# Attention and FFN in one kernel: wide matmuls issued as four column quarters that share rounds with PV, with other buffer rings and another split of the exponential

## The chip, the cores and the metric

The kernel runs on one core of a Trainium2 chip. The metric is the device time of one launch in microseconds (us); the median of three runs is shown. In the profile PE is the tensor engine (matmuls), PEld its weight loads, DVE the vector engine, ACT the scalar engine, POOL a third elementwise engine, SP the engine that issues most transfers.

## The reference

For x of 2048 rows and 512 columns the kernel computes x + attention(xn) + FFN(xn), with xn the layer norm of x. Attention has 32 query heads of size 16 and one shared key and value head. The FFN has 1792 inner columns.

```
xn = layernorm(x)
q, k, v = xn @ wq, xn @ wk, xn @ wv            # 32 heads of 16; one head of 16; one of 16
o = softmax(q @ k.T / 4) @ v                   # per head, all 2048 keys
out = x + o @ wo + gelu_tanh(xn @ w1 + b1) @ w2 + b2
```

## The kernel before

**Tiles and stages.** After a prologue (layer norm, transposes, K, V, the first Q) the main loop goes over 4 blocks of 512 queries. In each block there are 8 head groups of 4 heads, and in each group 16 key tiles of 128 keys: 64 score tiles of 128 keys by 512 queries, 2,048 in all. Three tiles make a *score group* (683 groups). `scores` (L620 to L635) issues its three matmuls of 17 rows, one per head in its own row quarter of the array, into three of six PSUM banks. The banks alternate, so the scores of group u+2 have to wait until group u has been read.

**Exponential on two engines.** ACT evaluates exp for all three tiles of a group, or for two (`exp`, L640, activation at L650), into E, a ring of 12 slots. The third tile then goes to DVE, which builds the exponential as a sum of five shifted integer approximations: a first pass from PSUM (`p1`, L666) and, per batch of up to three tiles, four shifts (L680). ACT tiles give one PV matmul each, DVE tiles five.

**PV.** `pv_mm` (L669 to L672) multiplies by V, 32 columns wide: head j uses column quarter j of the array and accumulates in one PSUM bank, pO. At the end of a head group DVE copies pO out (`o_evac`, L693), small transfers on SP turn the denominators round, and DVE writes the normalized oT (L704). PV of the next group must wait for the copy.

**Side work.** Q projections of the next block (`q_group`), the first FFN matmul (`h_mm`, L744) with the GELU chain, and the output blocks (`out_tile`: 14 matmuls with w2 in `y_mm`, 8 with wo in `wo_mm`) all write PSUM bank 7 with full-array matmuls of 128 by 512 through the helper `mm` (L403). A table of `at(u, ...)` calls says behind which exponential each becomes available.

**What sets the order.** A planner (`Prog.schedule`, L109) simulates five engines with given costs and writes each engine's order down; at run time an engine takes its instructions in exactly that order, with semaphore waits. On PE it prefers what is due first, stays on PV for up to 12 matmuls (4 with scores waiting), and puts a filler, a matmul with zeros (L886), where it sees PE idle for over 0.25 us while PV is open. DVE's share is an accumulator: 0.7 of the groups, always the third tile, never in the last 7 tiles of a head group.

## Time and profile before

| | |
|---|---|
| median of three runs | 901.55 us (899.56 to 901.85) |
| profiled execution, its own time | 904.14 us |
| its span, first to last instruction | 902.4 us |
| mean granted PE clock | 0.977 |
| first exponential starts, last ends | 44.1 us, 885.7 us |
| busy: PE, ACT, DVE | 861.9, 787.2, 784.7 us |
| score matmuls | 2,048 |
| PV matmuls from E, from DVE tiles | 1,602 and 2,230 |
| exponentials on ACT of three and of two tiles | 236 and 447 |
| fillers | 101 |

Busy times are unions of an engine's instructions. Matmul ends are modelled by the profiler, so starts are the better guide on PE. A clock of 0.50 in a row means that the tensor engine was granted half of its pulses.

### The profile page before, as it was taken

The numbers are of one execution on the slowest core, as the hardware profiler recorded it, in microseconds if no ns is written. First come the engines' busy times: TensorE is split into PE (matmuls) and PEld (weight loads), VectorE is DVE, ScalarE is ACT, GpSimd is POOL, SyncE is SP. The second block draws the span as 40 slices with busy tenths as digits, with TensorE's granted clock in tenths as the row PEclk, the third lists the DMA queues.
The fourth block names the chain that finished last, engine by engine and source line by source line (L and its number), as shares of the span: only waits on it lengthen the run. The fifth ranks groups of instructions, "written<-read, shape, count | busy, mean of one in ns | idle before, by whom it ended". The sixth has DMA issues, their size and how long they took to land.

```text
span 902.4 us, 16691 instructions
## 1 busy us (share of the span) xinstructions
PE 861.9 (96%) x6893; PEld 259.5 (29%) x6893; DVE 784.7 (87%) x1498; ACT 787.2 (87%) x731; POOL 25.7 (3%) x51
## 2 busy tenths in 40 slices
PE   4799999999999999999999999999999999999997
PEld 2313322222222223233232222222222233223322
DVE  7359999989887679999998787999998777999984
ACT  3469999989898898999999988999989889999982
POOL 6030000000000000000000000000000000000000
PEclk9859999989999999999999999999999999999999
DMA  8000000000000000000000000000000000000000
GB/s 281 1 25 14 14 5 10 13 14 13 15 15 7 19 20 20 13 13 5 10 16 13 20 25 20 13 10 5 13 16 13 20 25 20 1 13 14 13 14 24
DMA packets 23958, 18.79 MB, mean 21 GB/s; under 512 B 12370, under 2 KB 19403, under 8 KB 23883
## 3 DMA queue, kind: packets, MB, share of 16 engines
q1 hardware_dynamic: 22826, 17.69, 6.6%
q8 instruction: 55, 0.90, 0.4%
q10 hardware_dynamic: 1056, 0.03, 0.1%
q14 instruction: 21, 0.16, 0.1%
HBM read 14.98 MB, written 2.35 MB: 19 GB/s over the span
## 4 chain that ended last, share of the span: by engine, by line
PE 70%; DVE 17%; ACT 12%; issue 1%; DMA 0%; DVEq 0%; ACTq 0%
PE pAll L670 30%; PE pAll L403 19%; PE pAll L633 18%; ACT E L650 10%; DVE Dt L666 5%; DVE Dt L680 5%; PE pAll L886 2%; DVE hb L748 2%; ACT xnT L493 1%; ACT ub L762 1%; DVE ub L759 1%; DVE ub L761 1%; DVE stats L452 1%; DVE Of L693 1%; DVE ub L764 0%
## 5 line engine op out<-in xcount | busy, mean ns | idle before, releaser
L650 ACT ACTIVATE E<-pAll 128x1024 bf16<-128x1024 f32 (+1 forms) x683 | 747.1, 1187 | 73.6 <-PE pAll L633 41.5
L666 DVE TENSOR_SCALAR Dt<-pAll 128x512 int16<-128x512 f32 x446 | 300.6, 686 | 77.1 <-PE pAll L633 75.2
L670 PE MATMUL pAll<-Dt,V 128*32 128x512 bf16 x2230 | 348.9, 391 | 0.1
L680 DVE TENSOR_SCALAR Dt<-Dt 128x1536 int16<-128x1536 int16 x636 | 299.0, 529 | 2.0 <-PE pAll L670 0.4
L670 PE MATMUL pAll<-E,V 128*32 128x512 bf16 x1602 | 295.4, 393 | 4.2 <-DVE Of L693 3.4
L633 PE MATMUL pAll<-QT,KT 17*128 17x512 bf16 x2048 | 267.3, 389 | 11.3 <-ACT E L650 8.7
L633 PEld LDWEIGHTS pAll<-QT,KT 17*128 17x128 bf16 x2048 | 65.9, 91 | 247.5 <-ACT E L650 147.8
L670 PEld LDWEIGHTS pAll<-Dt,V 128*32 128x32 bf16 x2230 | 94.6, 95 | 118.5 <-issue 66.6
L670 PEld LDWEIGHTS pAll<-E,V 128*32 128x32 bf16 x1602 | 70.6, 94 | 99.2 <-issue 59.0
L403 PE MATMUL pAll<-w_sb,ub 128*128 128x512 bf16 x224 | 71.0, 391 | 0.0
L403 PE MATMUL pAll<-xnT,w_sb 128*128 128x512 bf16 x224 | 66.6, 386 | 0.8 <-DVE hb L748 0.8
L748 DVE TENSOR_SCALAR hb<-pAll,b1T 128x512 bf16<-128x512 f32 x56 | 41.8, 746 | 1.3 <-PE pAll L403 1.3
L403 PE MATMUL pAll<-xnT,wqp 128*128 128x512 bf16 x128 | 40.4, 403 | 0.1
L403 PE MATMUL pAll<-wop,oT 128*128 128x512 bf16 x128 | 37.6, 383 | 2.6 <-DVE x_sb L797 1.8
L886 PE MATMUL pAll<-xnT,zeros 128*128 128x512 bf16 x101 | 35.0, 389 | 0.0
L403 PEld LDWEIGHTS pAll<-w_sb,ub 128*128 128x128 bf16 x224 | 18.1, 98 | 38.7 <-issue 29.6
L762 ACT ACTIVATE ub<-ub 128x1536 bf16<-128x1536 bf16 (+1 forms) x20 | 28.2, 1410 | 0.0
L403 PEld LDWEIGHTS pAll<-xnT,w_sb 128*128 128x128 bf16 x224 | 16.1, 97 | 34.5 <-issue 15.3
L521 DVE CAST QT<-pAll 128x512 bf16<-128x512 f32 x32 | 22.0, 688 | 1.3 <-PE pAll L403 1.0
L490 PE MATMUL pAll<-ident,ub 128*128 128x128 bf16 x64 | 9.1, 306 | 14.1 <-POOL ub L476 10.5
L693 DVE COPY Of<-pAll 128x512 f32<-128x512 f32 x31 | 21.2, 683 | 0.0
L704 DVE TENSOR_TENSOR oT<-Of,rbc 128x512 bf16<-128x512 f32 x31 | 21.2, 683 | 0.0
(91 smaller groups left out, 260.7 us busy)
## 6 DMA issues: line engine op xcount, KB each, us to landing
rbc<-rden_rows SPq DMA_DIRECT2D x124, 64.0 KB, 2.0
w_sb<-in_B_w_dram SPq DMA_DIRECT2D x2, 1792.0 KB, 12.0
x_sb<-in_A_x_dram SPq DMA_DIRECT2D x8, 256.0 KB, 4.5
out_dram<-x_sb SPq DMA_DIRECT2D x16, 128.0 KB, 1.7
ub<-in_A_wq_dram SPq DMA_DIRECT2D x1, 512.0 KB, 6.3
wop<-in_A_wo_dram SPq DMA_DIRECT2D x4, 128.0 KB, 2.8
den<-Of SPq DMA_DIRECT2D x31, 8.0 KB
rden_rows<-den SPq DMA_DIRECT2D x31, 8.0 KB, 1.4
```

The source lines that it names most:

```text
L403: return add("pe", lambda e: e.matmul(o, l, rh, start=start, stop=stop, **kw), r, w, occ=occ, lat=0.23, allow=allow)
L521: dve(lambda e: e.tensor_copy(QT[:, pq, hq, :], bank(bk)), w=[B(bk), ("QT", pq, hq)] + [("QTm", pq, hq, j) for j in range(4)], **kw)
L633: ins = e.matmul(o, l, rh, start=True, stop=True, tile_position=(q0, 0))
L650: exps.append(act(lambda e: e.activation(E[:, s0:s0 + na, :], bank(3 * x, na).rearrange("p (a n) -> p a n", a=na), ACT.Exp, scale=LN2 / 12 ...
L666: dve(lambda e: e.tensor_scalar(Dt[:, KZ, s, :], bank(bk), float(127 * 128) + SPL_D, SPL_MIN, ALU.add, ALU.max), w=[B(bk), ("D", s, KZ)], ...
L670: add("pe", lambda e, a, b: e.matmul(pO[32 * j:32 * j + 32, :], V1[:, v, kt, :], rhs, start=a, stop=b, tile_position=(0, 32 * j)), r=r + [ ...
L680: dve(lambda e, k=k: e.tensor_scalar(Dt[:, k, s0:s0 + n, :], Dt[:, KZ, s0:s0 + n, :], float(SPL_K[k]), None, ALU.add), r=[("D", s0 + i, KZ ...
L693: dve(lambda e: e.tensor_copy(Of[:, i, :], pO), w=["O", ("Of", i)], allow=0.0)
L704: onorm[gg] = dve(lambda e: e.tensor_tensor(oT[:, tb % 2, g, :], Of[:, i, :], rbc[:, i, :], ALU.mult), r=[("Of", i)] + [("rbc", i, j) for ...
L748: dve(lambda e: e.tensor_scalar(hb[:, ft % 6, :], pM, b1T[:, ft:ft + 1], None, ALU.add), r=["b1T"], w=[B(7), ("h", ft % 6)])
L762: act(lambda e: e.activation(uu, uu, ACT.Tanh, scale=GELU_K), r=uk, w=uk, n=c, allow=2.5, kind="tanh")
L886: pr.filler = lambda e: e.matmul(pO, zeros[:], xnT[:, 0, 0:TBW], start=False, stop=False, skip_group_check=True)
```

## The change

**Quarters.** A new helper `mm4` issues each wide matmul of the side work as four, each with 32 of the 128 weight columns, into its own column quarter. They have the shape of PV, are marked "side", and may stand between PV matmuls. A few (one Q group and the prologue) stay wide.

**Planner.** `pick_pe` is new: in the quarter shape it fills free quarters, goes to scores as soon as they are ready and one matmul of the visit is done, and waits 0.1 us for scores that are nearly ready. A change of shape now costs 0.1 us in the plan; latencies are a little longer. No fillers.

**Rings.** Q has one slot per head group in place of two; O is a ring of ten in place of two times eight; E has 20 slots in place of 12, the DVE tiles 8 in place of 6. Squares for the Q norm get slots of their own.

**Times of availability.** Q projections of a block come as pairs over the block before (and, for the last pair, over the block itself) with 16 sets of four small transfers in place of 6 sets; output blocks come from 3 groups on, the FFN over a longer stretch.

**Split.** Which tiles DVE takes follows a running balance of ACT and DVE load with the side work's costs; first or third tile may go, none in the last 10 of a head group.

```diff
+SWITCH = 0.1
-D_RATE = 0.7
-D_TAIL = 7
+SWITCH = 0.1
+
+ETA = 0.97
+D_LEAD = 0.0
+D_PEN = 0.3
+D_TAIL = 10
 D_FIRST = 3
-FILL_GAP = 0.25
-PV_MIN = 6
-PV_MAX = 12
-PV_S = 4
+FILL_GAP = 0
+PV_MIN = 2
+PV_S = 1
+P1_ALLOW = -20.0
+EV_ALLOW = -2.0
+S_WAIT = 0.1
+P_WAIT = 0.0
+NE_ND_KB = (20,8,3)
...
+    def pick_pe(self, t, cand, allr, mode, visit, cgbusy):
+        S = [o for o in cand if o.kind == "S"]
+        rest = [o for o in cand if o.kind != "S"]
+        nxt = min([o.rdy for o in allr if o.kind == "S"] + [t + 9.0])
+        due = lambda o: (o.rdy + o.allow, o.idx)
+        if mode == "col":
+            end = max(cgbusy)
+            if t < end - 0.01:
+                if t < end - 0.216 + 0.03:
+                    c = [o for o in rest if o.tag is not None and cgbusy[o.tag[1]] <= t]
+                    if c:
+                        return min(c, key=due)
+                return end
+            if S and visit >= PV_S:
+                return S[0]
+            if rest:
+                n = len({o.tag[1] for o in rest if o.tag})
+                if nxt - t < S_WAIT and not S and n < 4:
+                    return None
+                if n >= PV_MIN or not S:
+                    return min(rest, key=due)
+            return S[0] if S else None
+        if S:
+            return S[0]
+        if not rest or nxt - t < S_WAIT:
+            return None
+        n = len({o.tag[1] for o in rest if o.tag})
+        if n >= PV_MIN or n == 0 or min(o.rdy + o.allow for o in rest) <= t:
+            return min(rest, key=due)
+        return None
...
+                op = self.pick_pe(t, cand, ready["pe"], mode, visit, cgbusy)
+                if op is None or isinstance(op, float):
+                    free["pe"] = t + 0.03 if op is None else op
+                    continue
...
+                if op.kind in ("pv", "side"):
                     cg = op.tag[1]
                     st = max(t, cgbusy[cg], free["pe"])
                     if mode != "col":
-                        st += 0.08
+                        st = max([t, pend + SWITCH] + [c + SWITCH for c in cgbusy])
                     op.start = st
-                    cgbusy[cg] = st + 0.215
-                    op.end = st + 0.055
+                    cgbusy[cg] = st + 0.216
+                    op.end = st + 0.006
                     op.vis = st + op.occ + op.lat
                     mode = "col"
                     g = op.tag[0]
...
-    NE, ND, KB = 12, 6, 3
+    NE, ND, KB = NE_ND_KB
+    NOT = 10
...
+        def mm4(o, l, rh, start, stop, r=(), w=(), allow=1.5):
+            for j in range(4):
+                c = slice(32 * j, 32 * j + 32)
+                add("pe", lambda e, c=c, j=j: e.matmul(o[c, :], l[:, c], rh, start=start, stop=stop,
+                                                       tile_position=(0, 32 * j)),
+                    r, [(k, j) for k in w] + [k for k in w if k != B(7)], occ=0.216, lat=0.23, allow=allow, kind="side", tag=(None, j))
+
+        M4 = [(("bank", 7), j) for j in range(4)]
...
-        def q_proj(tb, hq, bk, **kw):
+        def q_proj(tb, hq, bk, f=None):
             for d in range(DT):
-                mm(bank(bk), wqp[:, d, 4 * hq:4 * hq + 4, :].rearrange("p a n -> p (a n)"),
-                   xnT[:, d, tb * TBW:(tb + 1) * TBW], d == 0, d == DT - 1, r=["wqp", ("xnT", tb)], w=[B(bk)], **kw)
+                (f or mm)(bank(bk), wqp[:, d, 4 * hq:4 * hq + 4, :].rearrange("p a n -> p (a n)"),
+                   xnT[:, d, tb * TBW:(tb + 1) * TBW], d == 0, d == DT - 1, r=["wqp", ("xnT", tb)], w=[B(bk)])
+
...
-                w=[B(bk), ("D", s, KZ)], allow=0.0, kind="p1")
+                w=[B(bk), ("D", s, KZ)], allow=P1_ALLOW, kind="p1")
...
-            onorm[gg] = dve(lambda e: e.tensor_tensor(oT[:, tb % 2, g, :], Of[:, i, :], rbc[:, i, :], ALU.mult),
-                            r=[("Of", i)] + [("rbc", i, j) for j in range(HG)], w=[("oT", tb % 2, g)], allow=3.0)
+            onorm[gg] = dve(lambda e: e.tensor_tensor(oT[:, gg % NOT, :], Of[:, i, :], rbc[:, i, :], ALU.mult),
+                            r=[("Of", i)] + [("rbc", i, j) for j in range(HG)], w=[("oT", gg % NOT)], allow=3.0)
...
         def h_mm(tb, ft):
             for d in range(DT):
-                mm(pM, w1_sb[:, d, ft * P:(ft + 1) * P], xnT[:, d, tb * TBW:(tb + 1) * TBW], d == 0, d == DT - 1,
+                mm4(pM, w1_sb[:, d, ft * P:(ft + 1) * P], xnT[:, d, tb * TBW:(tb + 1) * TBW], d == 0, d == DT - 1,
                    r=["w1", ("xnT", tb)], w=[B(7)])
             dve(lambda e: e.tensor_scalar(hb[:, ft % 6, :], pM, b1T[:, ft:ft + 1], None, ALU.add),
-                r=["b1T"], w=[B(7), ("h", ft % 6)])
+                r=["b1T"], w=M4 + [("h", ft % 6)], allow=EV_ALLOW)
...
+        def q_pair(tb, hqs, u):
+            for i, hq in enumerate(hqs):
+                at(u + 1.5 * i, lambda tb=tb, hq=hq: q_group(tb, [hq], {}), 0.93)
+            at(u + 1.5 * len(hqs), lambda tb=tb, hqs=hqs: q_m(tb, list(hqs)), 0.6)
+
+        q_pair(0, (1,), 0)
+        q_pair(0, (2, 3), 3)
+        q_pair(0, (4, 5), 10)
+        q_pair(0, (6, 7), 30)
+        at(14, b1_col)
...
-            a, b = (30, 118) if tb < NTB - 1 else (42, 112)
+                    at(u0 + 3 + 9 * i, lambda tb=tb, i=i: out_tile(tb - 1, i), 0.6)
+                q_pair(tb, (6, 7), u0 + 50)
+            a, b = (40, 165) if tb < NTB - 1 else (38, 128)
             if tb == 0:
-                a = 12
...
+                for k in range(3):
+                    q_pair(tb + 1, (2 * k, 2 * k + 1), u0 + 46 + 42.7 * k)
...
+        COST_D = 0.6 + 4 * (0.133 + 0.065 / KB)
+        load = [0.0] * (NU + 1)
+        for u, _, _, c in side:
+            load[min(NU, max(0, int(u)))] += c
+        for gg in range(1, NTB * NGR):
+            load[gg * TPG // 3] += 1.5
+        act_t, dve_t = D_LEAD, 0.0
+        par, cgn = [0, 0], [0] * HG
+        for u in range(NU):
+            dve_t += load[u]
+            ok = [t for t in (3 * u, 3 * u + 2) if t < NTILE and t % TPG < TPG - D_TAIL]
+            pen = D_PEN * (par[u % 2] - par[1 - u % 2])
+            d = bool(ok) and u >= D_FIRST and dve_t + COST_D + pen <= act_t + 0.9
+            if d:
+                t = min(ok, key=lambda t: (cgn[t % HG], -t))
+                is_d[t] = True
+                cgn[t % HG] += 1
+                par[u % 2] += 1
+                dve_t += COST_D
+            act_t += ETA * (0.904 if d else 1.331)
+            dve_t = max(dve_t, act_t - 6.0)
+        for t in range(NTILE):
+            if is_d[t]:
+                last_d[t // TPG] = t
 
```

Where the change moves work on PE, first within an output block, in the second block of queries (near score group 212). L633 and L673 are scores, L670 and L713 PV, L403 and L451 side work; `w_sb,ub` is the second FFN matmul, `wop,oT` the output projection. Before:

```order
L633 MATMUL pAll<-QT,KT 128x512 x3
L403 MATMUL pAll<-w_sb,ub 128x512
L633 MATMUL pAll<-QT,KT 128x512 x3
L403 MATMUL pAll<-w_sb,ub 128x512 x4
L670 MATMUL pAll<-Dt,V 32x512 x3
L670 MATMUL pAll<-E,V 32x512
L633 MATMUL pAll<-QT,KT 128x512 x3
```

There, full-array matmuls stand alone between scores or ahead of PV. And in the change, at the same score groups:

```order
L673 MATMUL pAll<-QT,KT 128x512 x3
L713 MATMUL pAll<-E,V 32x512
L451 MATMUL pAll<-wop,oT 32x512
L451 MATMUL pAll<-w_sb,ub 32x512 x2
L451 MATMUL pAll<-wop,oT 32x512
L713 MATMUL pAll<-Dt,V 32x512
L713 MATMUL pAll<-E,V 32x512
L451 MATMUL pAll<-wop,oT 32x512
L713 MATMUL pAll<-E,V 32x512
L713 MATMUL pAll<-Dt,V 32x512
```

Between two scores everything now has the one shape 32x512, side work and PV mixed.

The second place is PE at the end of a head group late in the first block of queries (near score group 151), where PV of the next group waits for the copy of pO. Before (`hb,sel8R` is the Q norm):

```order
L633 MATMUL pAll<-QT,KT 128x512 x3
L403 MATMUL pAll<-hb,sel8R 32x512 x2
L633 MATMUL pAll<-QT,KT 128x512 x3
L403 MATMUL pAll<-hb,sel8R 32x512 x3
L633 MATMUL pAll<-QT,KT 128x512 x3
L670 MATMUL pAll<-E,V 32x512 x4
L633 MATMUL pAll<-QT,KT 128x512 x6
L670 MATMUL pAll<-E,V 32x512 x4
```

In the change:

```order
L673 MATMUL pAll<-QT,KT 128x512 x3
L713 MATMUL pAll<-Dt,V 32x512 x2
L713 MATMUL pAll<-E,V 32x512 x3
L673 MATMUL pAll<-QT,KT 128x512 x15
L713 MATMUL pAll<-E,V 32x512
L673 MATMUL pAll<-QT,KT 128x512 x3
L713 MATMUL pAll<-E,V 32x512 x5
L713 MATMUL pAll<-Dt,V 32x512 x6
```

Five score groups stand there with no other matmul between them, in place of two.

The third place is ACT from score group 125 or so on. Before:

```order
L650 ACTIVATE E<-pAll 128x1024 x4
L650 ACTIVATE E<-pAll 128x1536
L650 ACTIVATE E<-pAll 128x1024 x3
L650 ACTIVATE E<-pAll 128x1536 x2
L650 ACTIVATE E<-pAll 128x1024 x4
```

In the change, over the same groups:

```order
L692 ACTIVATE E<-pAll 128x1536 x3
L692 ACTIVATE E<-pAll 128x1024 x4
L692 ACTIVATE E<-pAll 128x1536 x5
L692 ACTIVATE E<-pAll 128x1024 x2
L692 ACTIVATE E<-pAll 128x1536
```

Three-tile evaluations (1536) come in longer runs, and there are more of them.

More of the change, by code (lines that the diff above doesn't have):

```diff
@@ L128, in schedule @@
         visit = 0
+        pend = 0.0
         accn = {}
@@ L206, in schedule @@
                     op.vis = op.end + op.lat
-                    mode = "row" if op.kind == "S" else "full"
+                    if m == "col":
+                        cgbusy = [op.end] * 4
+                    mode = m
             else:
@@ L634, in fn @@
                 return ins
-            return add("pe", fn, r, [B(3 * x + i) for i in range(3)], occ=0.32, lat=0.18, allow=-1.0, kind="S")
+            return add("pe", fn, r, [B(3 * x + i) for i in range(3)], occ=0.216, lat=0.22, allow=-1.0, kind="S")
         eptr = [0]
```

167 lines of the change are left out of this document (73 added, 94 removed).

## The prediction

> **What bounds the kernel now.** I read the page's first part, then the timeline of the tensor engine, then stretches of the main loop.
>
> ```profile
> span 902.4 us, 16691 instructions
> PE 861.9 (96%) x6893; PEld 259.5 (29%) x6893; DVE 784.7 (87%) x1498; ACT 787.2 (87%) x731; POOL 25.7 (3%) x51
> ```
>
> PE looks busy for 96% of the span, but its ends are modelled, so I price it by starts. In the timeline, columns are start, length, engine, line, operation, count:
>
> ```profile
> 408.47 0.39 PE L633 MATMUL pAll<-QT,KT 17*128 17x512 bf16 x3
> 408.79 0.39 PE L670 MATMUL pAll<-Dt,V 128*32 128x512 bf16 x1
> 408.85 0.40 PE L670 MATMUL pAll<-E,V 128*32 128x512 bf16 x3
> 409.18 0.39 PE L633 MATMUL pAll<-QT,KT 17*128 17x512 bf16 x3
> 409.50 0.39 PE L886 MATMUL pAll<-xnT,zeros 128*128 128x512 bf16 x1
> 409.82 0.39 PE L670 MATMUL pAll<-Dt,V 128*32 128x512 bf16 x1
> ...
> 897.27 1.47 PE L403 MATMUL pAll<-wop,oT 128*128 128x512 bf16 x6 [0.79 <-DVE x_sb L797]
> ```
>
> Six matmuls of one shape take 1.47 us: (1.47 - 0.39) / 5 = 0.216 us from start to start. That is one round of the array. Three score matmuls (17 rows each), or four PV matmuls of four different column quarters, share one round. Each change of shape (score, full array, quarter) costs more: score at 408.47, quarter at 408.79, that is 0.32, and score, full, quarter at 409.18, 409.50, 409.82 again 0.32 each. So a change costs 0.32 - 0.216 = 0.10 us.
>
> With these two prices I counted the built program's order in 32 stretches of 21 score groups (672 of 683 groups). PE needs 672 score rounds, 1,363 quarter rounds (3,790 tiles; quarters that come unevenly leave holes) and 748 full rounds, with 1,598 changes: 2,783 x 0.216 + 1,598 x 0.10 = 760.9 us. The other two engines I price by instructions that follow without a gap:
>
> ```profile
> L650 ACT ACTIVATE E<-pAll 128x1024 bf16<-128x1024 f32 x5 | 4.7, 1073 | 0.0
> ```
>
> ```profile
> L650 ACT ACTIVATE E<-pAll 128x1536 bf16<-128x1536 f32 x4 | 5.5, 1458 | 0.0
> ```
>
> ```profile
> 128.25 1.96 DVE L680 TENSOR_SCALAR Dt<-Dt 128x1536 int16<-128x1536 int16 x4
> ...
> 410.23 1.29 DVE L666 TENSOR_SCALAR Dt<-pAll 128x512 int16<-128x512 f32 x2
> ```
>
> An exponential of two tiles takes (4.7 - 1.07) / 4 = 0.91 us of ACT, one of three (5.5 - 1.46) / 3 = 1.35; I use 0.92 and 1.33, within the rounding of 4.7 and 5.5. On DVE a shift of three tiles takes (1.96 - 0.55) / 3 = 0.47 us and a first pass 1.29 - 0.69 = 0.60. By stretch, I set the largest of the three needs against the time from one stretch's first exponential to the next's. Rows of eight stretches (window, length, then busy time by engine, PEclk after POOL):
>
> ```profile
> 306.60:333.00 26.40, 26.40 (x219) 7.79 (x211) 21.14 (x41) 23.07 (x23) 0.00 (x0) 1.00 0.07 22
> 668.50:691.20 22.70, 21.70 (x190) 6.08 (x187) 19.14 (x38) 22.70 (x23) 0.00 (x0) 1.00 0.06 16
> 99.60:123.60 24.00, 24.00 (x204) 7.26 (x202) 23.31 (x44) 22.80 (x23) 0.00 (x0) 1.00 0.05 14
> 44.10:75.90 31.80, 29.83 (x186) 6.44 (x184) 21.48 (x40) 24.32 (x22) 8.75 (x9) 0.68 0.06 17
> 174.20:201.30 27.10, 25.54 (x201) 6.99 (x199) 24.65 (x48) 24.36 (x23) 0.00 (x0) 0.87 0.05 11
> 227.50:254.60 27.10, 25.35 (x204) 7.29 (x200) 22.49 (x44) 22.81 (x22) 0.00 (x0) 0.94 0.05 13
> 277.60:306.60 29.00, 27.58 (x213) 7.79 (x216) 19.04 (x37) 23.01 (x22) 0.00 (x0) 0.94 0.05 15
> 872.20:902.40 30.20, 23.97 (x167) 8.85 (x161) 17.60 (x35) 12.76 (x12) 0.00 (x0) 1.00 0.06 18
> ```
>
> The first took 26.4 us where PE needs 25.9 (95 rounds, 54 changes), the second 22.7 where ACT needs 22.6. Over the 28 stretches from 75.9 to 872.2 us that had the full clock, the time is 713.1 and the sum of largest needs 700.5: a factor of 1.018. So this count tells the time, and the bound changes by stretch: PE in 10 (250.4 us), DVE in 16 (406.2), ACT in 6 (140.1), in sum 796.8. Four stretches are longer than that factor allows, and in each the granted clock is below 1: the first by about 8.8 us (31.8 against a need of 23.0), the other three by 1.9, 3.6 and 3.1 (needs 24.8, 23.1, 25.4).
>
> **The change, part by part.** *Quarters.* These groups lose their full-array form:
>
> ```profile
> L403 PE MATMUL pAll<-w_sb,ub 128*128 128x512 bf16 x224 | 71.0, 391 | 0.0
> L403 PE MATMUL pAll<-xnT,w_sb 128*128 128x512 bf16 x224 | 66.6, 386 | 0.8 <-DVE hb L748 0.8
> L403 PE MATMUL pAll<-xnT,wqp 128*128 128x512 bf16 x128 | 40.4, 403 | 0.1
> L403 PE MATMUL pAll<-wop,oT 128*128 128x512 bf16 x128 | 37.6, 383 | 2.6 <-DVE x_sb L797 1.8
> L886 PE MATMUL pAll<-xnT,zeros 128*128 128x512 bf16 x101 | 35.0, 389 | 0.0
> ```
>
> The first four, less a few, become four tiles each. Packed alone they need as many rounds as before. But they stand in one visit with PV and fill its holes: in the same 672 groups the order has 672 score rounds, 1,824 quarter rounds (6,199 tiles) and 1 full round, with 1,244 changes. The 101 fillers are gone. 2,497 x 0.216 + 1,244 x 0.10 = 663.8 us: PE needs 97 us less. In the example stretch (groups 210 to 230) it falls from 25.9 to 88 x 0.216 + 40 x 0.10 = 23.0.
>
> A quarter's weight load has to fit under its round:
>
> ```profile
> 406.32 0.11 PEld L670 LDWEIGHTS pAll<-Dt,V 128*32 128x32 bf16 x4
> ```
>
> Four loads of a round take 0.11 us together, under 0.216, so I add nothing. The Trainium skill (TensorEngine Tiling, Incompatibilities under Restrictions and Gotchas) says that column tiling excludes fast weight load, which speaks against quartering the wide loads. By it alone, with 0.095 us added for each of 2,816 loads, the sum would rise by some 267 us; the row just shown is of such tiles and denies it.
>
> *Split between ACT and DVE.* Two-tile exponentials go from 441 to 410, three-tile ones from 231 to 262 (same groups): ACT's need rises by 31 x (1.33 - 0.92) = 12.8 us, to 750.5 with the tanh work. DVE loses 31 first passes (18.6 us) and, with fuller batches, about 17 us of shifts: 728.7 becomes 692.9. By stretch the largest need is now ACT's in 24 (572.1), DVE's in 5 (121.6), PE's in 3 (69.6): in sum 763.4, that is 33.4 less than before.
>
> *Rings.* Waits that the longer E ring and the DVE priority touch:
>
> ```profile
> DVE Dt L666 <- PE pAll L633: 75.2, 95, 3.2
> ACT E L650 <- PE pAll L670: 29.9, 30, 3.2
> ```
>
> The 30 waits of ACT for PV come at the ends of head groups, when twelve slots are full; twenty slots hold some eight exponentials. What this can give lies between 0 and 29.9 us, but most of it is in stretches that DVE or PE bounds, and ACT is behind them. I take 0 beyond the factor of 1.018. Single Q slots make a projection's copy wait for the last score of the old head group; it stands some 3 groups after that, and the result is read over 60 groups later: 0, and if late at most one wait of the page's size, 3.2 us. The 40 more small Q loads sit on SP among the reciprocal loads; one more landing of about 2.0 us ahead of a normalized O, which three output blocks wait for, is at most 6 us, and out tiles have other quarters to run under it: 0.
>
> ```profile
> rbc<-rden_rows SPq DMA_DIRECT2D x124, 64.0 KB, 2.0
> ```
>
> *Clock.* With no fillers, PE can fall idle. Rows before each fall of the clock, one low stretch that kept it, and the long cold start:
>
> ```profile
> 176.54:179.95 3.41, 1.87 (x17) 0.45 (x12) 3.41 (x7) 3.41 (x5) 0.00 (x0) 1.00 0.00 0
> 234.56:237.97 3.41, 1.66 (x19) 0.42 (x21) 3.36 (x7) 1.67 (x2) 0.00 (x0) 1.00 0.02 5
> 285.76:289.17 3.41, 1.99 (x26) 0.53 (x23) 3.41 (x7) 2.08 (x3) 0.00 (x0) 1.00 0.00 0
> 781.10:784.50 3.40, 2.32 (x17) 0.67 (x16) 3.40 (x6) 3.40 (x4) 0.00 (x0) 1.00 0.02 5
> 46.83:67.31 20.48, 20.33 (x99) 3.65 (x99) 12.52 (x23) 13.37 (x13) 6.59 (x7) 0.50 0.10 27
> ```
>
> With under 2.0 busy us of 3.41 the clock was 0.50 next; with 2.32 it stayed. In the new order, behind the first groups, 11 runs of three to five score groups stand with nothing between them; before there was none of three. Three groups on ACT's pace are over 3 us with under 1 us of PE work, so I count 11 falls. One cost 1.9 to 3.6 us before, mean 2.9, where PE had no slack. Now it has 12% (663.8 of 763.4). Lower bound 0, upper 3.6; I take 1.7, nearer to the mean than to 0: 19 us.
>
> **The sum.** 44.1 us up to the first exponential; first stretch 24.6 + 8.8 = 33.4; the other 31: (763.4 - 24.6) x 1.018 = 752.1; the end 30.2 (its window above); falls 19: 878.8 us of span. The profiled execution took 904.14 us for its 902.4, and the median of the runs is 901.55: 878.8 + 1.7 - 2.6 = 878 us.
>
> **Rivals.** *No falls.* The clock could hold: then the sum is 860 (859.8 - 0.9 is 859). For it: the count of 3.41 us windows is no rule, and their phase is chance. Against: three falls in the rows above. The longest idle gap at one of them was
>
> ```profile
> 237.95 0.62 PE L670 MATMUL pAll<-E,V 128*32 128x512 bf16 x4 [0.94 <-DVE Of L693]
> ```
>
> so 0.94 us. The Trainium skill (TensorE: Matmul & The Clock Gate, the table under Why this matters for your kernels) only forbids idle gaps above about 3 us; by that rule the runs, broken by scores, cost nothing and this rival holds. The trace disagrees with it.
>
> *Chained falls (slower).* At the start the clock stayed at 0.50 for 20.48 us and cost 8.8. PV that piled up behind a run meets a slow PE, scores stand behind it in PE's order, ACT starves. With six of 11 falls that long and five at 1.7: 859 + 53 + 8 = 920. It decides from five long ones: 859 + 44 = 903. Against: in three of four falls the clock came back within 6.9 us.
>
> *The gain doesn't arrive (same).* ACT-bound stretches may need a larger factor, since every score must come within one exponential: at 1.05 the sum is 738.8 x 1.05 + 33.4 + 44.1 + 30.2 + 19 = 902.
>
> **How the numbers follow.** Forecast (870 to 898 us) 0.53; no falls (under 870) 0.22; same 0.08; chained falls 0.17. Below 848 ACT would have to run without any loss in most stretches; above 908 lies about half of the slower case, so the range is 848 to 908 us. A measurement of this kernel tells 0.3% from no change: faster 0.75, same 0.08, slower 0.17.
>
> **What would show it.** PE's shape changes near 1,270 in place of 1,630, exponentials of 416 and 267, no row for fillers; stretches of 21 groups near 24 us with ACT busy over 95%; a mean granted clock near 0.94 with falls right behind long score runs (near groups 87, 151, 343, 496). Wrong, if ACT-bound stretches at full clock are over 1.03 of ACT's need, if quarter rounds start more than 0.23 us apart, or if a fall costs outside 0 to 3.6 us.

## The result and the profile after

The changed kernel took 875.22 us (median of four executions, 873.05 to 878.26), beside 901.7 us for the kernel before: a ratio of 0.969, 95% interval 0.961 to 0.977. The execution whose profile is shown took 878.26 us for a span of 876.4. It was the longest of the four, and its clock the lowest: 873.05 us came with a granted clock of 0.949, 873.8 with 0.947, 876.64 with 0.943, 878.26 with 0.934.

The page of the changed kernel: span, busy times, the granted clock in 40 slices, and the chain of waits by engine.

```profile
span 876.4 us, 20514 instructions
...
PE 801.6 (91%) x8766; PEld 238.4 (27%) x8768; DVE 751.7 (86%) x1429; ACT 788.6 (90%) x731; POOL 25.5 (3%) x51
...
PEclk9668998779889999999999999998889999999999
...
ACT 51%; PE 33%; DVE 14%; issue 1%; DMA 0%; DVEq 0%; ACTq 0%
```

PE's share of the span fell from 96% to 91%. The chain that ended last now runs half of its time through ACT. The clock row shows what was paid: most slices below 9 from 22 to 263 us, and three near 620.

The wide matmuls and the exponentials by shape, from the groups of instructions (count, then busy us and mean ns of one, then idle time before them):

```profile
L451 PE MATMUL pAll<-w_sb,ub 128*32 128x512 bf16 x896 | 111.0, 391 | 0.0
L451 PE MATMUL pAll<-xnT,w_sb 128*32 128x512 bf16 x896 | 81.2, 400 | 1.3 <-DVE hb L790 1.0
...
L692 ACT ACTIVATE E<-pAll 128x1024 bf16<-128x1024 f32 x416 | 416.0, 1133 | 20.5 <-PE pAll L673 19.9 <-PE pAll L713 0.4
L692 ACT ACTIVATE E<-pAll 128x1536 bf16<-128x1536 f32 x267 | 388.7, 1549 | 24.2 <-PE pAll L673 20.0 <-PE pAll L713 3.6
```

The quarters are there, four for each wide matmul (224 became 896). The exponentials are 416 of two tiles and 267 of three. Fillers have no row.

Now the windows of the changed kernel: three stretches of 21 score groups at full clock, three with falls of the clock, then the whole loop from the first exponential on (the 672 groups that were counted) and the end. The columns are window, length, busy time of PE, PEld, DVE, ACT, POOL with counts, granted clock, DMA share, GB/s.

```profile
205.20:228.60 23.40, 22.04 (x239) 6.50 (x235) 19.62 (x38) 23.40 (x22) 0.00 (x0) 1.00 0.05 14
744.90:769.30 24.40, 22.86 (x269) 6.22 (x273) 24.37 (x44) 24.40 (x24) 0.00 (x0) 1.00 0.05 14
301.70:326.70 25.00, 24.48 (x324) 7.40 (x316) 17.44 (x35) 24.04 (x22) 0.00 (x0) 1.00 0.08 18
...
44.70:74.10 29.40, 26.94 (x239) 6.74 (x237) 18.29 (x36) 25.39 (x22) 8.55 (x9) 0.77 0.07 20
124.50:152.30 27.80, 25.98 (x238) 6.92 (x227) 23.50 (x43) 25.27 (x23) 0.00 (x0) 0.88 0.04 11
177.90:205.20 27.30, 25.90 (x216) 6.07 (x208) 23.36 (x41) 24.19 (x23) 0.00 (x0) 0.75 0.06 12
...
44.70:846.40 801.70, 751.88 (x8254) 217.14 (x8256) 710.74 (x1332) 759.70 (x693) 8.55 (x9) 0.94 0.06 15
846.40:876.40 30.00, 24.26 (x350) 9.73 (x342) 17.82 (x34) 12.29 (x11) 0.00 (x0) 1.00 0.09 28
```

The same loop of the kernel before:

```profile
44.10:872.20 828.10, 811.64 (x6558) 238.46 (x6558) 743.94 (x1401) 757.75 (x692) 8.75 (x9) 0.98 0.05 14
```

All of the gain is in the loop: 828.1 to 801.6 us, 26.5 less (from unrounded starts; the row shows 801.70). Start (44.1, 44.7) and end (30.2, 30.0) stayed. By the prediction's count, the sum of the largest needs fell by 33.4 us (796.8 to 763.4). The 17 stretches that kept the full clock took 411.7 us for a need of 405.7, a factor of 1.015, like 1.018 before. In the 15 stretches with half clock the time above 1.018 of the need grew from 17.0 us (four stretches before) to 25.9. So 33.4 were won, 8.9 given back to the clock, and some 2.0 came from the factor: 33.4 x 0.018 = 0.6, as it stands on a smaller sum, and about 1.3, as it was itself a little smaller in the 17 stretches (405.7 x 1.018 = 413.0, where 411.7 were taken). 33.4 - 8.9 + 2.0 = 26.5.

The waits of ACT (us in total, times, longest) in the changed kernel:

```profile
ACT E L692 <- PE pAll L673: 39.9, 43, 2.8
...
ACT E L692 <- PE pAll L713: 4.0, 3, 2.6
```

The waits for PV to free an E slot went from 29.9 us to 4.0. Those for scores were 41.5 us in 66 waits and are 39.9 in 43: fewer and longer, most of them during a fall of the clock or right behind it.

One of the falls, first by windows of 3.41 us, then PE's timeline up to it (start, length, engine, line, operation, count, and in brackets the idle time before and what ended it):

```profile
232.70:236.11 3.41, 1.42 (x12) 0.32 (x9) 3.41 (x7) 3.41 (x5) 0.00 (x0) 1.00 0.00 0
236.11:239.52 3.41, 3.04 (x23) 0.81 (x27) 3.26 (x7) 3.41 (x4) 0.00 (x0) 0.50 0.02 5
```

```profile
232.55 0.39 PE L673 MATMUL pAll<-QT,KT 17*128 17x512 bf16 x3
233.47 0.39 PE L673 MATMUL pAll<-QT,KT 17*128 17x512 bf16 x3 [0.53 <-ACT E L692]
234.49 0.39 PE L673 MATMUL pAll<-QT,KT 17*128 17x512 bf16 x3 [0.63 <-DVE Dt L709]
235.30 0.39 PE L673 MATMUL pAll<-QT,KT 17*128 17x512 bf16 x3 [0.42 <-ACT E L692]
236.31 0.61 PE L673 MATMUL pAll<-QT,KT 17*128 17x512 bf16 x3 [0.61 <-ACT E L692]
```

This is the run of five score groups near group 151, the second place shown with the change. PE is busy for 1.42 us in the window, no idle gap is longer than 0.63 us (both by the modelled ends), and the next window has half of the pulses: the score matmul at 236.31 is 0.61 us long in place of 0.39.

### The profile page after: what moved, and what is told of

It is laid out like the page before. It is cut to its first block, busy times and chain, and to the rows that moved or that the text cites. A ratio compares the mean times of both kernels' runs of the same rounds, so it can differ in the third digit from the quotient of the medians.

```text
span 876.4 us, 20514 instructions
## 1 busy us (share of the span) xinstructions
PE 801.6 (91%) x8766; PEld 238.4 (27%) x8768; DVE 751.7 (86%) x1429; ACT 788.6 (90%) x731; POOL 25.5 (3%) x51
## 4 chain that ended last, share of the span: by engine, by line
ACT 51%; PE 33%; DVE 14%; issue 1%; DMA 0%; DVEq 0%; ACTq 0%
ACT E L692 49%; PE pAll L713 12%; PE pAll L451 10%; PE pAll L673 9%; DVE Dt L709 4%; DVE Dt L723 4%; PE pAll L445 2%; ACT ub L804 1%; DVE hb L790 1%; ACT xnT L544 1%; DVE stats L503 1%; DVE Of L736 0%; DVE ub L806 0%; DVE ub L801 0%; DVE ub L803 0%
## 5 line engine op out<-in xcount | busy, mean ns | idle before, releaser
L692 ACT ACTIVATE E<-pAll 128x1024 bf16<-128x1024 f32 (+1 forms) x683 | 751.2, 1295 | 44.7 <-PE pAll L673 39.9
L713 PE MATMUL pAll<-Dt,V 128*32 128x512 bf16 x2075 | 340.4, 401 | 2.5 <-DVE Dt L709 1.2
L709 DVE TENSOR_SCALAR Dt<-pAll 128x512 int16<-128x512 f32 x415 | 278.6, 682 | 60.7 <-PE pAll L673 56.6
L673 PE MATMUL pAll<-QT,KT 17*128 17x512 bf16 x2048 | 277.5, 400 | 43.5 <-ACT E L692 36.7
L713 PE MATMUL pAll<-E,V 128*32 128x512 bf16 x1633 | 309.1, 404 | 2.0 <-DVE Of L736 1.4
L723 DVE TENSOR_SCALAR Dt<-Dt 128x1536 int16<-128x1536 int16 (+2 forms) x588 | 282.8, 525 | 1.0
L673 PEld LDWEIGHTS pAll<-QT,KT 17*128 17x128 bf16 x2048 | 67.5, 91 | 329.2 <-ACT E L692 276.0
L713 PEld LDWEIGHTS pAll<-Dt,V 128*32 128x32 bf16 x2075 | 93.5, 98 | 98.4 <-issue 46.8
L451 PE MATMUL pAll<-w_sb,ub 128*32 128x512 bf16 x896 | 111.0, 391 | 0.0
L713 PEld LDWEIGHTS pAll<-E,V 128*32 128x32 bf16 x1633 | 74.3, 96 | 76.6 <-issue 56.4
L451 PE MATMUL pAll<-xnT,w_sb 128*32 128x512 bf16 x896 | 81.2, 400 | 1.3 <-DVE hb L790 1.0
L451 PE MATMUL pAll<-wop,oT 128*32 128x512 bf16 x512 | 70.1, 381 | 1.9 <-DVE x_sb L839 1.9
L451 PE MATMUL pAll<-xnT,wqp 128*32 128x512 bf16 x496 | 50.1, 442 | 0.5 <-DVE hb L790 0.3
L451 PEld LDWEIGHTS pAll<-w_sb,ub 128*32 128x32 bf16 x896 | 28.8, 96 | 25.6 <-issue 15.9
L575 DVE CAST QT<-pAll 128x512 bf16<-128x512 f32 x32 | 21.8, 683 | 13.9 <-PE pAll L451 10.1
L451 PEld LDWEIGHTS pAll<-xnT,w_sb 128*32 128x32 bf16 x896 | 21.2, 97 | 30.8 <-issue 15.1
L451 PEld LDWEIGHTS pAll<-wop,oT 128*32 128x32 bf16 x512 | 20.0, 95 | 15.7 <-issue 5.9
```

The source lines that it names most:

```text
L451: add("pe", lambda e, c=c, j=j: e.matmul(o[c, :], l[:, c], rh, start=start, stop=stop, tile_position=(0, 32 * j)), r, [(k, j) for k in w] ...
L575: dve(lambda e: e.tensor_copy(QT[:, hq, :], bank(bk)), w=[B(bk)] + [(B(bk), j) for j in range(4)] + [ ("QT", hq)] + [("QTm", hq, j) for j ...
L673: ins = e.matmul(o, l, rh, start=True, stop=True, tile_position=(q0, 0))
L692: exps.append(act(lambda e: e.activation(E[:, s0:s0 + na, :], bank(b0, na).rearrange("p (a n) -> p a n", a=na), ACT.Exp, scale=LN2 / 128.0 ...
L709: dve(lambda e: e.tensor_scalar(Dt[:, KZ, s, :], bank(bk), float(127 * 128) + SPL_D, SPL_MIN, ALU.add, ALU.max), w=[B(bk), ("D", s, KZ)], ...
L713: add("pe", lambda e, a, b: e.matmul(pO[32 * j:32 * j + 32, :], V1[:, v, kt, :], rhs, start=a, stop=b, tile_position=(0, 32 * j)), r=r + [ ...
```

## The experiments

The theory: (1) the changed order is bound by ACT, DVE or PE in turn, and the count of rounds and shape changes tells its time at full clock to within 2%; (2) what it loses against that is the clock, which falls behind runs of scores with nothing between them; (3) the quarters pay because they share rounds with PV. The rivals: ACT-bound stretches need a larger factor whatever the clock; the rest of the change (planner, rings, split, no fillers) brings the gain and the quarters little; and of what the clock reacts to, either the number of matmuls, their rows, or the lack of any full-array matmul. Each ratio below is against the kernel before on the same chip, with its 95% interval.

In the texts written ahead, "need" is the count of the prediction, summed over 32 stretches.

### One part undone at a time

**e1_wide**: the side work is issued as one wide matmul again, the rest of the change stays.

```diff
 def mm4(o, l, rh, start, stop, r=(), w=(), allow=1.5):
+    return mm(o, l, rh, start, stop, r, [(k, j) for k in w for j in range(4)] + [k for k in w if k != B(7)], allow=allow)
     for j in range(4):
```

> The change with its side matmuls left whole (128 columns, one in place of four quarters); planner, rings, times and split stay those of the change. Counted in its order with the prices of the prediction: PE needs 682.6 us in the first 672 groups (the change 663.8, before 760.9), sum of the largest needs by stretch 770.0 (763.4; 796.8). My theory (the largest need in each stretch sets the time, and most of PE's relief comes from fillers and badly placed shape changes that the new planner leaves out): about 7 us above the change, 882 us (876 to 889). Rival (the sharing of rounds by quarters is what gained): most of the gain is lost, 893 us or more.

Measured: 911.8 us, ratio 1.007 (1.003 to 1.011), clock 0.908. The forecast of 882 us was missed, and the rival's time came. Without the quarters the change, with a planner written for them, is no gain at all. But the count says little of it: the sum of needs is only 6.7 us larger (770.0). The loop is 25.8 us longer than the changed kernel's (827.4), and of that 20.7 is the excess of stretches with half clock, which were 150 us of the loop in place of 99. The end took 39.1 us in place of 30.0:

```profile
871.60:910.70 39.10, 30.79 (x197) 11.00 (x192) 20.41 (x38) 12.33 (x12) 0.00 (x0) 1.00 0.07 21
```

What wide matmuls would take with the new rings and a planner fitted to them was not tried.

**e2_oldsplit**: the tiles for DVE chosen as in the kernel before.

```diff
-        act_t, dve_t = D_LEAD, 0.0
-        par, cgn = [0, 0], [0] * HG
+        acc_d = 0.0
...
-            dve_t += load[u]
-            ok = [t for t in (3 * u, 3 * u + 2) if t < NTILE and t % TPG < TPG - D_TAIL]
...
+            t = 3 * u + 2
...
+            acc_d += 0.7
+            if acc_d >= 1.0 and t % TPG < TPG - 7 and u >= D_FIRST:
+                acc_d -= 1.0
```

> The change with the tiles of DVE chosen as before (0.7 of the groups, always the third tile, none in the last 7 of a head group); all else as in the change. Counted: ACT needs 735.3 us (the change 750.5), DVE 726.4 (692.9), sum of the largest needs 762.4 (763.4), runs of three or more score groups 15 (12). My theory (the largest need by stretch sets the time): no gain from the new split, 874 to 882 us. Rival A (ACT's need alone sets it now): 860 to 865. Rival B (the balance by load is a large part of the gain): 890 or more.

Measured: 905.62 us, ratio 1.001 (0.996 to 1.005). The forecast of 874 to 882 us was missed, and rival B's time came. Its needs sum to 762.4 us, nearly the changed kernel's 763.4, so by the count this part should be worth nothing. It cost 30 us: in the profiled execution (893.8 us of span) the end is 46.2 us in place of 30.0, and the loop 3.6 us longer with some 125 us at half clock. The rest, up to the median, comes with lower clocks (895.89 us at 0.922, 907.47 at 0.908).

**e3_ring12**: E, DVE and batch slots of 12, 6 and 3.

```diff
-NE_ND_KB = (20,8,3)
+NE_ND_KB = (12,6,3)
```

> The change with the old ring lengths (E 12 slots, DVE tiles 6); the planner orders anew for them. Counted: PE 688.8 us, sum of the largest needs 784.1 (the change 763.4). Here the waits of ACT for PV at the ends of head groups come back. My theory by the count: 21 us above the change, 896 us (888 to 905). The prediction took 0 for the rings themselves; a rival by that reading: within 4 us of the change, 872 to 879.

Measured: 933.38 us beside 903.8; one of four executions took 919.07 us at a clock of 0.912, the others 933.35 to 933.86 at 0.891, so no ratio is given, and 44 us above the changed kernel is the least it cost. The forecast was missed on the far side. The planner, with fewer slots, orders 111 more quarter rounds and 11 more shape changes (PE's need +25 us, the sum of the largest needs +21). ACT's waits, in the profiled execution of 933.86 us:

```profile
ACT E L692 <- PE pAll L713: 45.0, 28, 5.3
```

They are over ten times the changed kernel's 4.0 us, and more than before's 29.9. So the long ring is not a small help for this order. But the clock was at half for 184 us of this loop (99 in the changed kernel), and the runs don't separate what the waits cost from what the clock cost.

### What relief on PE is worth alone

**e6_before_nofill**: the kernel before, without its 101 fillers.

```diff
-FILL_GAP = 0.25
+FILL_GAP = 0
```

> The kernel before without its 101 fillers; all else as before, its planner orders anew. Counted in its order: PE needs 725.7 us in the first 672 groups (before 760.9), but the sum of the largest needs stays 796.3 (796.8), since PE's relief lies where DVE or ACT need as much. Theory (need by stretch plus falls of the clock): clock falls to about 0.93, at 0.3 us per us at half clock that costs some 25 us: 920 us (905 to 935). Rival (the fillers only take PE's time; PE bounds the kernel before): 875 to 890, most of what the change gained.

Measured: 906.73 us, ratio 1.003 (0.998 to 1.007), clock 0.970 in its profile: not the 920 us forecast, but within its range. PE's need fell by 35 us (760.9 to 725.7), the sum of largest needs by 0.5, the time by nothing. This is as the count has it: a shorter PE need is worth only what it takes from stretches that PE bounds, and the fillers stood elsewhere. The clock fell less than expected: seven falls in place of four.

### What the clock reacts to

**e4_dup3**: the changed order, but where a score group follows another directly (50 places), its three matmuls are issued three times.

```diff
+pe = [o for o in pr.ops if o.eng == "pe"]
+for o1, o2 in zip(pe, pe[1:]):
+    if o1.kind == o2.kind == "S":
+        o2.fn = (lambda e, f=o2.fn: [f(e) for _ in range(3)][-1])
```

> The change, and where score groups follow each other on PE with nothing between, from the second on, the three score matmuls are issued three times over the same banks (same values), so that PE streams 0.65 us in place of 0.22 in each. Theory of the falls (windows with under 2 busy us lower the clock, and the slow PE costs ACT time afterwards): mean clock 0.97 or more, time 858 to 867 us, the repeats costing back up to 0.2 us at some 50 places. Rival (those stretches are long because ACT starves at the ends of head groups, whatever the clock): clock up, time 873 or more. Second rival (the falls have another cause): clock stays near 0.94.

Measured: 894.74 us, ratio 0.989 (0.986 to 0.992), clock 0.925. Missed: 300 more score matmuls did not hold the clock, and the kernel became 20 us slower than the changed one. Its windows at the same fall:

```profile
235.90:239.31 3.41, 2.49 (x29) 0.69 (x27) 3.41 (x6) 3.23 (x4) 0.00 (x0) 1.00 0.00 0
239.31:242.72 3.41, 3.41 (x22) 0.71 (x16) 2.29 (x6) 3.10 (x3) 0.00 (x0) 0.50 0.00 0
```

PE was busy 2.49 of 3.41 us, more than the 2.32 with which the kernel before kept its clock, and fell. So 2.49 busy us, most of them of 17-row score matmuls, did not keep the clock where 2.32 of a mix with full-array matmuls did.

**e5_hold**: the changed order with 57 full-array matmuls added where the plan leaves PE idle and bank 7 is free. Their results are overwritten.

```diff
+n = min(3, int((nxt[id(o)].start - o.start - o.occ - 0.3) / 0.216))
+for _ in range(n):
+    f = _Op()
...
+    f.fn = lambda e: e.matmul(pM, ident[:], xnT[:, 0, 0:TBW], start=True, stop=True)
+    out.append(f)
```

> The change, its order kept, with 57 full-array matmuls (128 by 512) into PSUM bank 7 added on PE at places where the plan leaves PE idle for over 0.5 us and no side work is open there, mostly within runs of score groups; nobody reads them. They cover 8 of the 12 runs of three or more. Theory (the clock falls where few quarter and full matmuls stream in a 3.41 us window, score matmuls hardly count; a fall costs ACT time afterwards): falls drop from 15 to about 7, mean clock about 0.965, time 15 us below the change, 860 us (855 to 867). Rival (stretches with runs are long because ACT starves there): clock up, time 872 or more. Second rival (extra matmuls delay scores, as the repeated scores did): 880 or more.

Measured: 865.24 us, ratio 0.956 (0.951 to 0.962), clock 0.957, eight falls in place of 15. As forecast. The loop is 12 us shorter than the changed kernel's. The same 21 groups that took 27.3 us there:

```profile
169.40:192.80 23.40, 22.01 (x218) 6.14 (x213) 22.98 (x41) 23.40 (x23) 0.00 (x0) 1.00 0.05 13
```

23.4 us, ACT without a gap. So the 57 added matmuls make the kernel faster: the loss in this stretch was the clock's, and not ACT's own.

**e12_full_ahead**: no matmuls in bank 7, but one full-array matmul ahead of the scores at the 50 places of e4_dup3, into the bank that the scores then overwrite.

```diff
+pe = [o for o in pr.ops if o.eng == "pe"]
+for o1, o2 in zip(pe, pe[1:]):
+    if o1.kind == o2.kind == "S":
+        o2.fn = (lambda e, f=o2.fn, x=o2.tag[1]: (e.matmul(bank(3 * x), ident[:], xnT[:, 0, 0:TBW],
+                                                           start=True, stop=True), f(e))[1])
```

> The change, its order kept; at the same 50 places where the repeated scores stood (score groups that follow another with nothing between), one full-array matmul ahead of the scores, into a bank that they overwrite. It delays the scores by 0.42 us (one round, two shape changes), the repeats did by 0.43 us; so PE is as long busy and only the shape differs. Theory (score matmuls hardly count for the clock, full ones do): fewer falls than the 12 of the repeats, clock 0.955 or more, 862 to 875 us. Rival (delay and busy time decide, not the shape): clock near 0.925 and some 893 us, as with the repeats.

Measured: 880.2 us, ratio 0.974 (0.964 to 0.985), clock 0.936 in its profile, 11 falls. The theory's 862 to 875 us was missed, and so were the rival's 893. One full-array matmul with its two shape changes delays the scores as long as two extra score rounds, and the kernel is 15 us faster than e4_dup3 (on another chip); but the clock was not held, and the kernel is not faster than the changed one. At the same place:

```profile
236.10:239.50 3.40, 2.45 (x16) 0.68 (x15) 3.40 (x6) 3.31 (x5) 0.00 (x0) 1.00 0.00 0
239.50:242.91 3.41, 2.77 (x15) 0.55 (x16) 2.72 (x6) 3.41 (x4) 0.00 (x0) 0.50 0.02 5
```

The clock was 0.50 next here too. So neither busy time nor the presence of full-array matmuls tells by itself when the clock falls. What it counts stays open.

### Holding the clock in every run of score groups

**e8_hold_all** and **e9_hold_all2**: e5_hold with one, or two, full-array matmuls ahead of the 24 score groups that still follow another score group directly.

```diff
+pe = [o for o in out if o.eng == "pe"]
+for o1, o2 in zip(pe, pe[1:]):
+    if o1.kind == o2.kind == "S":
+        o2.fn = (lambda e, f=o2.fn, x=o2.tag[1]: ([e.matmul(bank(3 * x + k), ident[:], xnT[:, 0, 0:TBW], start=True, stop=True)
+                                                      for k in range(2)], f(e))[1])
```

These are e9's lines; e8 has one matmul in place of `range(2)`.

> The kernel with held clock (57 full-array matmuls into bank 7, 865 us, clock 0.957) and, in each score group that still follows another with nothing between (24), one full-array matmul ahead of its scores into the bank that they overwrite. No run of score groups is left. Theory (falls cost about 0.3 us per us at half clock; 54 us of them are left after the start): falls 2 or fewer, clock 0.975, some 0.2 us of delay at each of 24 places: 853 us (847 to 860). By the count alone, with the factor of the full-clock stretches and no falls: 44.2 + 763.4 x 1.012 + 30 = 847. Rival (the delay of scores eats it): 865 or more.

> As the run before, with two full-array matmuls ahead of each of those 24 score groups in place of one. Theory: one matmul per group gives some 0.22 us of 1.1, near the limit of what kept the clock; two are safely above it. If falls are left with one, this run has fewer and is equal or faster, 850 to 858 us; if one already holds the clock, the second only delays scores by 0.2 us more at 24 places, up to 5 us slower.

Measured: e8 862.33 us, ratio 0.956 (0.953 to 0.959), clock 0.974; e9 863.54, ratio 0.954 (0.947 to 0.961), with executions of 855.6 us at a clock of 0.986, 859.49 at 0.983, 867.58 at 0.966 and 869.16 at 0.924. Both missed their forecasts (847 to 860 and 850 to 858) on the slow side. In e8's profile no run of score groups is left, and yet the clock falls five times in the loop, where two or fewer were expected: other places make it fall too. The profile of e9 is its fastest execution, with a single fall in the loop (6.8 us). Its loop and its end:

```profile
45.50:823.80 778.30, 735.43 (x8326) 219.96 (x8360) 708.74 (x1331) 758.05 (x693) 8.54 (x9) 1.00 0.06 15
823.80:853.80 30.00, 24.28 (x350) 9.74 (x342) 18.21 (x35) 12.31 (x11) 0.00 (x0) 1.00 0.09 28
```

This is the changed kernel nearly without falls. Its loop is 23.3 us shorter than the changed kernel's 801.6, against the 25.9 us that the stretches with half clock had there; and its 31 stretches at full clock took 753.0 us for a need of 738.3, a factor of 1.020. So nearly all that the changed kernel lost against its count was the clock. The rival that ACT-bound stretches need a factor of 1.05 falls, as a mean over them. e8 has the steadier times (862.11 to 863.43): 4.4% below the kernel before, where the change has 3.1%. The ratios of e5, e8 and e9 (0.956, 0.956, 0.954) can't be told apart.

### The parts again, with the added matmuls

**e7_wide_hold**: e1_wide with 50 matmuls as in e5_hold. **e10_wide_hold_all**: also with those of e8_hold_all. **e11_oldsplit_hold_all**: e2_oldsplit with both kinds. The edits are the ones shown.

> The kernel with whole side matmuls (the change's planner, rings, times and split), which took 912 us at a clock of 0.91, plus 50 full-array matmuls into PSUM bank 7 where its plan leaves PE idle, as in the run before. Theory (of its 37 us over the change, 7 are need by stretch, 9 its end, some 19 falls of the clock, which quarters of side work in the score runs would have prevented): 892 us (885 to 900), clock 0.95. Rival (whole matmuls cost by their place and shape changes, not by the clock): 905 or more whatever the clock.

> Whole side matmuls with the clock held in both ways (79 matmuls in bank 7 or ahead of scores). It tells what quarters are worth when the clock does not fall. Theory by the count: sum of the largest needs 772.1 against 763.8 with quarters, and an end some 9 us longer: 17 us above the quarters with held clock, 870 us (863 to 880), clock 0.97. Rival (whole matmuls cost by holding up scores, which no count by stretch sees): 885 or more at that clock.

> The change with the old choice of DVE tiles and the clock held in both ways. Theory by the count: sum of the largest needs 762.6 against 763.8, and an end some 16 us longer (its last stretch leaves more for DVE and PE behind the last exponential): 868 us (860 to 876). Rival (ACT's need, 15 us lower, counts once the clock is held): 855 or less. Rival (an uneven split costs within stretches): 880 or more.

Measured: e7 897.96 us, ratio 0.992 (0.988 to 0.996), clock between 0.93 and 0.95, as forecast. e10 895.71, ratio 0.992 (0.988 to 0.996), clock 0.950: the forecast of 870 us at a clock of 0.97 was missed in both. e11 876.9, ratio 0.975 (0.969 to 0.982), clock 0.961: 0.9 us above its range. With the holds, wide matmuls are some 32 us slower than quarters (ratios 0.992 and 0.956, on one chip), but their clock was not held as well. Split by the profiles of e10 and e8 (894.4 and 862.11 us): the loop 15.5 us (801.8 and 786.3), of which 8.3 are needs (772.1 and 763.8) and the rest goes with half clock (72 us of it in the loop, beside 38); the end 15.2 us (45.3, at a clock of 0.84, and 30.1). The old split costs 14.6 us, and nothing of it in the loop (786.0 and 786.3), as the count has it: all is in the end. That end, and its matmuls with w2 by group:

```profile
827.00:873.40 46.40, 35.21 (x482) 13.77 (x474) 23.78 (x45) 14.72 (x13) 0.00 (x0) 0.94 0.06 18
```

```profile
L452 PE MATMUL pAll<-w_sb,ub 128*32 128x512 bf16 x224 | 18.4, 410 | 1.8 <-DVE x_sb L835 1.8
```

The same group in the end of the changed kernel:

```profile
L451 PE MATMUL pAll<-w_sb,ub 128*32 128x512 bf16 x87 | 11.8, 381 | 0.0
```

224 quarters are four whole output blocks, and 87 is one and a half. So the old split leaves more side work behind the last exponential, where nothing runs beside it. In the end of e10 there are 42 wide matmuls with w2, that is three blocks, where the kernel before has 21.

## Why the prediction was right, point by point

The forecast was 878 us; 875.22 was measured, and the profiled execution took 878.26. The sum gave a span of 878.8; it was 876.4.

- **The price of a round and of a change of shape held.** Shape changes in the trace went from 1,630 to 1,270, just as forecast, and nearly all quarter rounds start 0.215 to 0.230 us apart at full clock, within the limit of 0.23. So four different weight loads add at most some 0.014 us to a round.
- **The bound moved to ACT, and the factor stayed on the whole.** 205.20 to 228.60 took just ACT's need, 744.90 to 769.30 as well; the sum over the 17 stretches at full clock is 1.015 of the largest needs, and in all fourteen profiled programs this factor lies between 1.00 and 1.03. The rival "the gain doesn't arrive" is denied by this, and once more by e9_hold_all2. But 301.70 to 326.70 took 1.05 of ACT's need, and the next stretch 1.09: 23.70 us (row below), where its 15 two-tile and 6 three-tile exponentials need 21.8. Both are above the 1.03 that the prediction set as a sign of error, so the largest need doesn't tell the time of each single stretch. In both PE has much to do as well (busy for 24.48 and 23.17 us); that this is why they are longer is not shown.

```profile
326.70:350.40 23.70, 23.17 (x267) 6.97 (x266) 20.69 (x40) 22.16 (x23) 0.00 (x0) 1.00 0.04 13
```

- **The rings were taken at 0 beyond the factor.** For the changed kernel against the one before, this fits the sum. But it isn't what the long ring is worth: with twelve slots the change, ordered anew, loses 44 us or more, a part of it through the clock (e3_ring12). The sum could use 0 only because the rest of the order had been made with twenty slots.
- **The first stretch was forecast at 33.4 us and took 29.4.** It was at a clock of 0.77 where it had 0.68 before; half clock held for 13.7 us in place of 20.5. Above 1.018 of the need (24.6 and 23.0) it cost 4.4 us in place of 8.4; the prediction's 8.8 stands above the need alone. Carrying the old length and price over was the one term of the sum that failed clearly. That the fall is cheaper because PE now has slack fits, but was not tested alone.
- **Falls: 11 at 1.7 us forecast, 14 found (beside the start) at 1.5.** (25.9 - 4.4) / 14 = 1.5, so 21.5 us where the sum had 19. (PE's slack, on which the 1.7 rests, is 13%, not 12%: 663.8 of 763.4.) The two errors of the clock, at the start and in the loop, nearly cancel: 27.8 us forecast, 25.9 found. Holding the clock (e5, e8, e9) shows the cause of the loss, and that the "no falls" rival, at 860 us, would have been about right for its case: e9's execution at 0.986 took 855.6, the more so as the start's fall went too. Chained falls of some 20 us did not come: four of the 15 lasted 10.2 to 13.7 us, the others 6.8 or less.
- **The count of falls was in part luck.** It went by runs of three or more score groups, but of the 14 falls only six begin within such a run or right behind it, and three such runs (at 433, 534 and 583 us) kept the clock. Of the four places named, those near groups 151, 343 and 496 have their fall in the run or behind it (at 236.1, 461.4 and 638.9 us); near group 87 the clock had fallen at 154.2 us, before the run began. The other eight falls stand where scores alternate with a few quarters, as in the first pair of rows here; the second pair is a run that kept the clock. So theory (2) is right in that the loss is the clock's, and only in part right in where the clock falls.

```profile
181.49:184.90 3.41, 2.35 (x23) 0.65 (x23) 3.38 (x7) 3.41 (x5) 0.00 (x0) 1.00 0.02 2
184.90:188.31 3.41, 3.41 (x24) 0.72 (x21) 2.64 (x7) 3.41 (x4) 0.00 (x0) 0.50 0.01 2
...
533.10:536.51 3.41, 2.48 (x29) 0.64 (x26) 3.40 (x7) 3.41 (x5) 0.00 (x0) 1.00 0.02 5
536.51:539.92 3.41, 3.41 (x57) 1.19 (x53) 3.41 (x7) 3.02 (x3) 0.00 (x0) 1.00 0.02 2
```

- **"Under 2.0 busy us of 3.41" was no rule.** In the changed kernel seven of the 15 windows before falls hold more, up to 2.37 us, and every other window at full clock in the loop holds 2.48 or more. So a limit near 2.4 would have told its falls. But that is no rule either: e4_dup3 (2.49) and e12_full_ahead (2.45) fell, and in e9_hold_all2 a window with 2.18 kept the clock (rows below). The Trainium skill's limit for idle gaps of about 3 us (TensorE: Matmul & The Clock Gate, the table under Why this matters for your kernels) would have let none of these falls come; at 236.11 the longest gap was 0.63 us, so the trace denies it, as it did before.

```profile
441.69:445.10 3.41, 2.18 (x13) 0.68 (x14) 3.15 (x7) 3.41 (x5) 0.00 (x0) 1.00 0.00 0
445.10:448.51 3.41, 3.00 (x39) 0.95 (x38) 3.41 (x7) 3.41 (x5) 0.00 (x0) 1.00 0.00 0
```

- **What the sum had by luck.** It took the quarters' gain to be 97 us of PE need turned into 33.4 us of the largest needs. But 78 of the 97 us come without quarters, from the planner, the fillers left out and the rest of the change: with wide matmuls the new planner's order has a PE need of 682.6 us (760.9 before), and the largest needs sum to 770.0, only 6.7 us more than with quarters. So theory (3), the shared rounds, accounts for 18.8 us of PE's need and 6.7 of the sum. e1_wide loses 36 us all the same, through the clock and the end. And the old split, nearly equal by the count, loses 30. So the count prices an order that is given, its end included; it doesn't tell which part of the change the gain belongs to. The end at 30.2 us was simply carried over, and was right because the new order leaves as little behind as the old one.

## What to carry to other kernels

Price the tensor engine by rounds and changes of shape in short stretches, and take the largest need among the engines in each: a relief on one engine is worth only what it takes from the stretches which that engine bounds (35 us of PE's need were worth nothing in e6_before_nofill). Add up many stretches, since a single one can be 5 to 9% off. Then look at what the new slack does: an engine with slack may lose its clock, and some matmuls whose results nobody reads, put where it idles, can be worth more (some 13 us here, from 875.2 to 862.3) than they cost. Count the work that a new order leaves for the end as well, where nothing runs beside it.

## What was unexpected of the hardware

- The granted clock falls with PE idle for no longer than 0.63 us at a time (the windows at 232.70 and 236.11), and the half clock comes in pieces of 3.4 us (3.4, 6.8, 10.2 or 13.7 in the changed kernel).
- Streaming more is not enough: windows with 2.45 and 2.49 busy us of 3.41 were followed by half clock, one with full-array matmuls among the scores, one with scores nearly alone, while 2.32 us were enough in the kernel before. None of the rules tried over all traces (busy time, rows, number of matmuls, longest gap) separates the windows. Of 3,015 windows of 3.41 us at full clock, 136 were followed by half clock; the best limit on busy time is wrong for 62 of them, the best on the rounds that start in a window (0.216 us each) for 45. What the clock counts stays open.
- A microsecond of half clock costs 0.25 to 0.5 us of time, over the thirteen programs with more than one fall: least where PE has slack (0.26 in the changed kernel), most where it has none (0.50 before). The clock also differs from one execution to the next, and longer times mostly go with lower clocks: 855.6, 859.49 and 867.58 us in e9_hold_all2 at 0.986, 0.983 and 0.966. Its fourth execution does not fit: 869.16 us at 0.924 would be some 70 us more at half clock for 1.6 us of time. It has no profile, and this stays open.
